# A TensorE-bound attention and MLP kernel: list-scheduled program order, DMA transposes from the seventh head pair on, exp bias as an immediate

## The chip, the cores and the metric

The kernel runs on one core of a Trainium2 chip. The metric is the device time of one execution in microseconds. A profile's span (first to last instruction) is about 2 us shorter than the time that goes with it. Engines: PE is TensorE (matmul), PEld its weight loads, DVE is VectorE, ACT is ScalarE, POOL is GpSimd, SP is SyncE, which issues DMAs here.

## The reference

Block-sparse attention over 4 batches, 8 heads, 768 tokens and head size 64 is followed by a residual token-and-channel MLP.

```python
scores = scale * q @ k.T                      # per batch and head
scores = where(mask, scores, -1e9)            # 32x32 blocks: band, edges, 3 sampled
attn = softmax(scores); x = attn @ v          # heads side by side: (4, 768, 512)
a1 = alpha1 * x + beta1
u = x + lam * (w_tok @ a1)                    # token mix, 768 x 768
a2 = alpha2 * u + beta2
out = u + lam * (relu(a2 @ w_ch1) @ w_ch2)    # channel MLP, 512 -> 2048 -> 512
```

## The kernel before

Work goes by pairs of heads, 16 in all, four to a batch. The scores of a pair are made in nine units of 1024 columns (`qk`), each goes through one exp on ScalarE (`eT`), and a second set of matmuls (`pv`) multiplies with v. The mask is added by 24 extra contraction rows of the operands: `kx` carries a block indicator, `qx` the bias of that block. After a pair come normalization, the token mix (`tok`), and a transposed copy `uT` of the result. Once a batch has all four pairs, its channel MLP runs in groups `ch1` (into `hts`, by relu) and `ch2` (into the output). All matmuls of MLP and token mix are fillers between attention units.

Both transposed operands come from TensorE, through a shared pair of PSUM buffers `mm`, and VectorE copies them out:

```python
    def prepare(b, n):                      # q and k of the next pair
        q2, k2, v2 = loaded.pop((b, n))
        ...
        for i, src in enumerate((q2, k2)):  # cast beside each other into rel
            nc.vector.tensor_copy(out=rel[:, :, :, i * D : (i + 1) * D], in_=...)
        yield
        for a in range(2):
            flat = transposes(rel, a)       # 6 matmuls against identity, into mm
            h = (2 * n + a) % NQB
            nc.vector.tensor_copy(out=qx[h][0:D, :], in_=flat[0:D, :])
            nc.vector.tensor_copy(out=kx[h][0:D, :], in_=flat[D:P, :])
            yield
```

```python
    def pair_mix(b, n):                     # cut to its end
        ...
        up = mm_tile([P, NT, P], BF)
        for t in range(NT):
            nc.tensor.transpose(up[:, t, :], ub[:, t, :], identb[:])
        nc.vector.tensor_copy(out=uTs[b][:, n, :], in_=up[:].rearrange("p o c -> p (o c)"))
```

The order is written by hand: a loop over the 144 units emits one `qk`, the `pv` of two units earlier, at most one piece of token mix, and channel groups against a credit of time. At the end `pin_order` makes the emitted order binding for every engine.

```python
    for i in range(len(units) + LAG):       # cut
        emit_qk(b, n, u)
        if u == 5: prep = prepare(*pairs[pi + 1])
        if prep is not None and u in (5, 7, 0): next(prep, None)
        ...
        if i >= NS: spent += filler(C1 if i % 2 else C2)
        ... pv of unit i - LAG ...
        spent += mix_next(i)
        if i >= NS: spent += filler(1e9)
```

The exp takes its bias from a 128x1 tile: `nc.scalar.activation(eT[:], sps[:], AF.Exp, bias=expb[:], scale=SCALE)`.

The softmax here doesn't subtract the row's maximum and nothing guards it: scores larger than these inputs give would overflow.

## Time and profile before

357.29 us is the median of three runs (352.35 to 357.5).

From the page of the kernel before: the head, some rows of the 40 slices of the span (busy tenths; PEclk is the granted TensorE clock), the chain that ended last (a name with q is a sequencer), and groups (busy us, mean ns of one, idle time before them and who ended it).

```profile
span 355.1 us, 7814 instructions
PE 333.2 (94%) x3375; PEld 220.2 (62%) x3410; DVE 210.8 (59%) x416; ACT 193.7 (55%) x213; POOL 43.4 (12%) x67
...
PE   7989998989899999999999999999999999999995
...
PEclk9999997789999999999999999999999999999999
...
PE 78%; DVE 15%; ACT 3%; issue 2%; DMA 1%; ACTq 0%; DVEq 0%
...
L299 ACT ACTIVATE eT<-sps,expb 128x1024 f16<-128x1024 f32 x144 | 157.5, 1114 | 91.4 <-PE sps L290 91.3
...
L225 PE MATMUL mm<-identb,rel 128*128 128x128 bf16 x192 | 17.3, 230 | 0.6 <-ACT hts L409 0.6
```

TensorE bounds the kernel: it is 94% busy and makes up 78% of the chain. ScalarE's exp is 1114 ns, but ScalarE waits for TensorE for 91 us, so it has room except at the start (18.5 of 20 us busy from 20 to 40 us).

Busy time of pipelined matmuls overlaps, and so says little about how much time could be won. The distance between two starts says more. The 128-column matmuls of L225 above have a mean of 230 ns each, but in the timeline such a matmul is followed after 56 ns, one of 384 after 163 ns, one of 512 after 216 ns, one of 65 after about 29 ns. I call the sum of these distances over all matmuls of the program the floor, and every start that comes later than its floor allows, an excess.

| before, us | floor | start to 50 us | 50 to 100 us | 100 to 290 us | rest | span |
|---|---|---|---|---|---|---|
| | 317.5 | 13.1 | 13.4 | 6.9 | 4.1 | 355.1 |

(Worked out from all starts in the trace; excess in each stretch; the first column of excess includes the 1.2 us before the first matmul; "rest" is nearly all the time after the last matmul. Matmuls missing from a trace, 35 here, are put back by their floor. Sums agree within 0.2 us.)

What TensorE waited for longest, in the view of waits (us in all, times, longest):

```profile
PE mm L401 <- DVE uT L383: 3.3, 6, 0.7
PE mm L382 <- DVE ub L375: 1.8, 1, 1.8
PE mm L464 <- DVE be2b L459: 1.4, 1, 1.4
```

Stretches of 20 us, in the view of windows (busy us of each engine with the number of instructions, clock, DMA share, GB/s; the share adds up packet times that can overlap, so it can exceed 1):

```profile
40.00:60.00 20.00, 18.14 (x292) 14.39 (x290) 17.23 (x39) 16.73 (x16) 8.57 (x12) 0.93 1.26 203
60.00:80.00 20.00, 17.39 (x218) 14.34 (x217) 12.93 (x26) 9.36 (x9) 2.14 (x3) 0.73 0.41 61
120.00:140.00 20.00, 19.54 (x205) 13.04 (x207) 12.87 (x26) 12.55 (x14) 2.14 (x3) 1.00 0.26 44
```

From 60 to 80 us the mean clock is 0.73. The clock record has half clock (starts of 128 columns are then 107 ns apart instead of 56) for 10.2 us from 57.2 us and for 3.4 us from 74.3 us. The two single waits above (1.4 us at 54.7 us, 1.8 us at 71.8 us) stand just before these stretches. From 100 us on there is a regular loss, 6.9 us in all. Its largest part are the six waits for uT in the list: `ch1` is queued in TensorE's order behind a q/k transpose, and waits for an `mm` buffer that the copy of uT has not yet freed (0.9 us of excess at 144, 184, 225 and 265 us).

### The profile page before, as it was taken

How to read it: one execution, taken by the hardware profiler on the slowest of the kernel's cores; microseconds unless marked ns; L12 is line 12 of the kernel's file. 1: busy time of each engine (PE TensorE's matmuls, PEld its weight loads, DVE VectorE, ACT ScalarE, POOL GpSimd, SP SyncE). 2: the span in 40 equal slices, each digit the busy share in tenths (PEclk: the TensorE clock that was granted, in tenths of full speed). 3: DMA queues.
4: the chain of work that ended last, by engine and by line, in shares of the span. 5: the costliest groups of instructions: out<-in, count | busy, mean ns of one | idle time of the engine just before them, and what ended most of it. 6: DMA issues, size and time to landing. Idle time of an engine off the chain costs nothing.

```text
span 355.1 us, 7814 instructions
## 1 busy us (share of the span) xinstructions
PE 333.2 (94%) x3375; PEld 220.2 (62%) x3410; DVE 210.8 (59%) x416; ACT 193.7 (55%) x213; POOL 43.4 (12%) x67
## 2 busy tenths in 40 slices
PE   7989998989899999999999999999999999999995
PEld 3578776765575666566666667566666656555542
DVE  3399996576785665665674755665674655242321
ACT  3898996545756656556556646566656630212110
POOL 4666334010010101002010000000000000000000
PEclk9999997789999999999999999999999999999999
DMA  5999999503132240603242000000000000001012
GB/s 132 203 220 224 207 207 201 86 3 45 22 41 30 49 78 2 99 30 50 50 54 44 31 32 0 31 31 0 31 32 0 31 31 30 31 30 61 30 40 79
DMA packets 20518, 23.34 MB, mean 66 GB/s; under 512 B 1756, under 2 KB 16260, under 8 KB 20484
## 3 DMA queue, kind: packets, MB, share of 16 engines
q0 software_dynamic: 15984, 15.47, 27.4%
q1 hardware_dynamic: 4284, 7.14, 5.6%
q8 instruction: 26, 0.43, 0.5%
q10 hardware_dynamic: 216, 0.24, 0.2%
q14 instruction: 8, 0.07, 0.1%
HBM read 30.86 MB, written 6.29 MB: 105 GB/s over the span
## 4 chain that ended last, share of the span: by engine, by line
PE 78%; DVE 15%; ACT 3%; issue 2%; DMA 1%; ACTq 0%; DVEq 0%
PE cp L433 20%; PE mm L401 19%; PE sps L290 14%; PE mm L363 8%; PE ops L311 7%; PE sps L401 3%; PE ops L433 3%; PE mm L225 2%; DVE x_sb L328 2%; ACT eT L299 2%; DVE a1p L350 2%; DVE a1p L353 1%; DVE kx L266 1%; DVE ub L375 1%; DVE x_sb L374 1%
## 5 line engine op out<-in xcount | busy, mean ns | idle before, releaser
L299 ACT ACTIVATE eT<-sps,expb 128x1024 f16<-128x1024 f32 x144 | 157.5, 1114 | 91.4 <-PE sps L290 91.3
L290 PE MATMUL sps<-qx,kx 88*128 88x512 bf16 (+1 forms) x384 | 91.0, 341 | 1.7 <-DVE kx L266 0.9
L401 PE MATMUL mm<-uT,w1b 128*128 128x384 bf16 x436 | 87.6, 325 | 4.7 <-DVE uT L383 3.3
L433 PE MATMUL cp<-w2b,hts 128*128 128x512 bf16 x303 | 78.6, 379 | 2.5 <-DVE ot L442 0.8
L401 PEld LDWEIGHTS <-w1b 128*128 128x128 bf16 x512 | 48.2, 97 | 38.9 <-issue 4.8
L311 PEld LDWEIGHTS <-eT 128*128 128x128 f16 x1152 | 56.0, 100 | 24.5 <-DVE x_sb L328 1.9
L409 ACT ACTIVATE hts<-mm,b1t 128x384 bf16<-128x384 f32 x64 | 37.0, 578 | 50.7 <-PE mm L401 50.0
L433 PEld LDWEIGHTS <-hts 128*128 128x128 bf16 x384 | 36.2, 97 | 34.2 <-issue 1.0
L311 PE MATMUL ops<-vext,eT 128*128 128x65 f16 x1008 | 53.8, 197 | 0.9 <-DVE x_sb L328 0.8
L290 PEld LDWEIGHTS <-kx 88*128 88x128 bf16 x384 | 32.4, 101 | 15.5 <-issue 2.7
L363 PE MATMUL mm<-a1p,wtokT 128*128 128x128 bf16 x576 | 41.2, 225 | 0.8 <-ACT hts L409 0.8
L363 PEld LDWEIGHTS <-wtokT 128*128 128x128 bf16 x576 | 34.8, 101 | 1.4 <-issue 0.9
L413 DVE TENSOR_SCALAR hts<-mm,b1t 128x384 bf16<-128x384 f32 x45 | 27.7, 616 | 9.1 <-PE mm L401 8.5
L374 DVE TENSOR_TENSOR x_sb<-x_sb,mm 128x384 f32<-128x384 f32 (+1 forms) x35 | 18.1, 518 | 24.3 <-PE mm L363 24.0
L265 DVE COPY qx<-mm 64x768 bf16<-64x768 bf16 x30 | 16.4, 547 | 26.2 <-PE mm L225 26.1
L442 DVE TENSOR_TENSOR ot<-x_sb,cp 128x512 f32<-128x512 f32 x21 | 14.4, 685 | 18.6 <-PE cp L433 18.6
L413 DVE TENSOR_SCALAR hts<-sps,b1t 128x384 bf16<-128x384 f32 x19 | 11.7, 617 | 20.2 <-PE sps L401 20.2
L171 POOL DMA_DIRECT2D q<-in_q_dram x15 | 10.7, 712 | 90.5 <-DVE rel L257 83.5
L325 DVE RECIPROCAL rcp<-ops 128x6 f32<-128x6 f32 x28 | 5.4, 193 | 23.2 <-PE ops L311 23.2
L375 DVE TENSOR_TENSOR ub<-x_sb,a_bc 128x384 bf16<-128x384 f32 (+1 forms) x35 | 18.3, 524 | 1.2
L225 PEld LDWEIGHTS <-rel 128*128 128x128 bf16 x192 | 14.4, 103 | 6.4 <-issue 2.9
L225 PE MATMUL mm<-identb,rel 128*128 128x128 bf16 x192 | 17.3, 230 | 0.6 <-ACT hts L409 0.6
(64 smaller groups left out, 210.4 us busy)
## 6 DMA issues: line engine op xcount, KB each, us to landing
out_dram<-ot SPq DMA_DIRECT2D x24, 256.0 KB, 2.0
v<-in_v_dram POOLq DMA_DIRECT2D x16, 192.0 KB, 5.2
q<-in_q_dram POOLq DMA_DIRECT2D x15, 192.0 KB, 6.0
k<-in_k_dram POOLq DMA_DIRECT2D x15, 192.0 KB, 6.2
w1b<-in_moe_w_ch_dram POOLq DMA_DIRECT2D x4, 512.0 KB, 10.4
w2b<-in_moe_w_ch_dram POOLq DMA_DIRECT2D x4, 512.0 KB, 15.6
wtk<-in_moe_w_tok_dram POOLq DMA_DIRECT2D x3, 384.0 KB, 8.0
a_bc<-in_moe_alpha_dram POOLq DMA_DIRECT2D x2, 256.0 KB, 8.8
```

What stands on the lines that cost most here:

```text
L225: nc.tensor.transpose(tps[:, o, :], rel[:, a, o, :], identb[:])
L265: nc.vector.tensor_copy(out=qx[h][0:D, :], in_=flat[0:D, :])
L290: nc.tensor.matmul(sps[:, f - u * UN : f - u * UN + w], kx[h][0:KC, ts(jt, P)], qx[h][0:KC, c : c + w], start=True, stop=True,)
L299: nc.scalar.activation(eT[:], sps[:], AF.Exp, bias=expb[:], scale=SCALE)
L311: nc.tensor.matmul(ops[(b, n, a)][:, t * VW : t * VW + D + 1], eTs[(b, n, u)][:, ts(c, P)], vx[:, a, jt, 0 : D + 1], start=(r == 0), stop= ...
L363: nc.tensor.matmul(tp[:, j, :], wtokT[:, s, ts(m * g + j, P)], a1p[:, s, :], start=(s == 0), stop=(s == NT - 1),)
L374: nc.vector.tensor_tensor(out=sl, in0=sl, in1=tp[:], op=ALU.add)
L375: nc.vector.tensor_tensor(out=ub[:, gs, :], in0=sl, in1=bc(a2_bc, m), op=ALU.mult)
L401: nc.tensor.matmul(hp[:, 0:HS], w1b[:, dk, ts(f, P)], uTs[b][:, dk, ts(hf, HS)], start=(dk == 0), stop=(dk == 3),)
L409: nc.scalar.activation(hts[k][:, f, :], hp[:, 0:HS], AF.Relu, bias=b1t[:, f : f + 1], scale=1.0)
L413: nc.vector.tensor_scalar(out=hts[k][:, f, :], in0=hp[:, 0:HS], scalar1=b1t[:, f : f + 1], scalar2=0.0, op0=ALU.add, op1=ALU.max,)
L433: nc.tensor.matmul(cps[k][:], hts[k][:, nk, ts(m, P)], w2b[:, nk, :], start=(nk == 0), stop=(nk == 15),)
```

## The change

It takes transposes off TensorE from the seventh pair on, and replaces the hand-written order by one that a small simulation of the engines chooses when the program is built: jobs with durations, dependencies, priorities and buffer counts, each engine always taking the best job that is ready. The relu, which went to ScalarE and VectorE in turn, now goes to the one that the simulation finds free. The exp bias becomes an immediate, and the warm-up gets 3 + 2 more matmuls.

```diff
-LAG = 2
+NPE = 6
+LEAD = 12
...
-    keep_warm(7, 512)
+    keep_warm(10, 512)
...
-    keep_warm(5, P)
+    keep_warm(7, P)
...
-        nc.scalar.activation(eT[:], sps[:], AF.Exp, bias=expb[:], scale=SCALE)
+        nc.scalar.activation(eT[:], tl.pop(("sps", p, u))[:], AF.Exp, bias=EXPB, scale=SCALE)
...
+    qs = [pp.tile([P, 2, NT, P], BF, name=f"qs{i}", tag=f"qs{i}") for i in range(2)]
+    ks = [pp.tile([P, 2, NT, P], BF, name=f"ks{i}", tag=f"ks{i}") for i in range(2)]
...
+        else:                               # pairs NPE and later
+            cq = cast_job(p, 0, "q2", ring_of(p, 0), (3, p, 0), ("ring",), ring_jobs)
+            ck = cast_job(p, 1, "k2", ring_of(p, 1), (3, p, 1), (), [cq])
...
+                def xt(p=p, a=a, h=h):
+                    for src, dst in ((qs, qx), (ks, kx)):
+                        nc.sync.dma_start_transpose(
+                            dst[h % NQB][:].rearrange("p (o c) -> p o c", o=NT),
+                            src[p % 2][:, a, :, :].rearrange("p o c -> p (o c)"))
...
+        if b == 0:                          # uT by TensorE, as before
...
+        else:
+            def uxt(p=p, n=n, ut_tile=ut_tile):
+                nc.sync.dma_start_transpose(ut_tile()[:, n, :]..., tl["ub", p][:]...)
...
-    for i in range(len(units) + LAG):       # and all of the hand-written order
+    while left:                             # list scheduling: (gated, priority) among ready jobs
+        for e in ("PE", "ACT", "DVE", "LD", "XP", "ST"):
+            ...
+            free_at[e] = t + j.dur
```

`qs` and `ks` are two staging buffers for a pair each ("the ring"): VectorE casts into them and DMA transposes read them. They also hold the mask rows, so a transpose delivers a whole `qx` or `kx`. In the changed kernel 52 DMA transposes of 192 KB go through SyncE's queue, 40 for q and k and 12 for uT.

## The prediction

> **What bounds the kernel now.** TensorE: the page has it 94% busy over 355.1 us, and the chain of waits is 78% TensorE, 15% VectorE, 3% ScalarE. Busy time overlaps, so I use distances between starts in the timeline: 56 ns for a 128-column matmul, 163 ns for 384, 216 ns for 512, about 29 ns for 65. Over all 3410 matmuls in program order that is an issue floor of 317 us. The other 38 us, each start against its floor: 13 us before 50 us (first transfers, and the half clock that the clock record holds until 16.3 us); 14 us from 50 to 100 us; 6 to 8 us of stalls from 100 to 290 us (some 1 us per head pair); almost none in the channel-only end; 4 us after the last matmul. At 50 to 100 us the clock record drops to half for 10.2 us from 57.2 and 3.4 us from 74.3, beside TensorE waits of 1.4 us (for be2b) and 1.8 us (for ub): the clock costs about 7 us.
>
> **What the change removes.** 120 q/k transposes (192 to 72) and 72 uT transposes (96 to 24): 192 x 56 ns = 10.8 us of TensorE, all critical. Added: 5 warm-up matmuls and a mask product. New floor 308 us: -10 us, nearly certain. VectorE loses 40 qx/kx copies (547 ns) and 12 uT copies (555 ns), 28.5 of 211 us; it is 96% busy from 20 to 40 us, but those copies stay (pairs 1 to 5 keep TensorE), so this helps only latency later.
>
> The exp bias as an immediate: [...] The trace has 1114 ns with the pointer[...]. Only the first 36 units feel it (ScalarE 92% busy at 20 to 40 us)[...].
>
> **What it moves.** The list-scheduled order should take most per-pair stalls (no buffer held across transpose and copy) and bring the first ch1 matmul from 78.8 us to about 65. If TensorE stays dense at 50 to 80 us the half clock does not return. I credit 7 us at 50 to 100 us, 3 us in steady state, 2 us at the start.
>
> **What it adds.** 52 DMA transposes of 192 KB on SyncE's queue, about five per 20 us pair, in order with the stores. DMA engines are about a quarter busy after 80 us; four head buffers give about a pair (20 us) of slack, so 3 to 5 us of landing time is hidden. The trace before shows no DMA transpose: this is the least known part. Above 4 us each in series the queue would become the bound.
>
> **Sum.** 355 - 10 - 7 - 3 - 2 = 333 us of span; timed runs lie 2 us above the profile: **335 us**, range **325 to 346**. Faster by over 2%: 0.91; within 2%: 0.06; slower by over 2%: 0.03.
>
> **What would show it.** Right: transposes 72 + 24 + 36, [...]no half clock after the ramp, TensorE waits for DMA-written qx/kx/uT under 3 us in total, landing of a transpose under 5 us. Wrong: TensorE waiting on those each pair; a transpose on SyncE behind a store or a buffer, holding up uT; half-clock stretches at 50 to 80 us.
>
> **What would make it wrong.** Slow or serialized DMA transposes; a fixed order that mis-times VectorE, so that TensorE stalls behind one late copy; the clock dropping in some runs and not others (before's own runs spread over 5 us), which alone moves the result by 5 us.

What makes up the 2 us at the start is not broken down. That the clock costs about 7 us is an estimate, half of the 13.6 us that the clock record of before has at half clock from 57.2 and 74.3 us. The 3 to 5 us of landing time had no trace behind them; the medians measured in the changed kernel are 2.6 us (kx), 2.7 us (uT) and 5.1 us (qx).

## The result, and the profile after

336.44 us (333.47 to 338.76, four runs, one of them slow; the three fast ones have a median of 335.49) against 354.98 us of before in the same rounds. The ratio is 0.9462 with a 95% interval of 0.9366 to 0.9558. A ratio is the mean time of one kernel's fast runs over that of the other's of the same rounds, so it is not quite the ratio of the medians. A later control of six runs gave 336.76 us and 0.9443.

The same parts of the page of the changed kernel:

```profile
span 331.7 us, 7564 instructions
PE 316.0 (95%) x3229; PEld 204.6 (62%) x3229; DVE 172.7 (52%) x352; ACT 190.4 (57%) x230; POOL 45.4 (14%) x71
...
PE   7798999896999999999999999999999999999995
...
PEclk9999999999799999999999999999999999999999
...
PE 83%; DVE 4%; ACT 4%; DMA 3%; issue 2%; SPq 1%; POOL 1%; ACTq 0%; DVEq 0%
...
L596 ACT ACTIVATE eT<-sps 128x1024 f16<-128x1024 f32 x144 | 144.5, 1024 | 69.2 <-PE sps L583 67.8
```

The transposes that are left on TensorE, in the view of groups, and the DMA transposes in the list of DMA issues (count, us to landing):

```profile
L209 PE MATMUL mm<-identb,rel 128*128 128x128 bf16 x72 | 6.0, 219 | 1.9 <-DVE rel L467 1.9
L735 PE MATMUL mm<-identb,ub 128*128 128x128 bf16 x24 | 2.0, 219 | 0.0
```

```profile
qx<-qs SPq DMA_TRANSPOSE x20, 5.1
kx<-ks SPq DMA_TRANSPOSE x20, 2.6
...
uT<-ub SPq DMA_TRANSPOSE x12, 2.7
```

q/k transposes on TensorE fell from 192 to 72. VectorE's share of the chain falls from 15% to 4%. The windows (the last row is the stretch shown of before):

```profile
60.00:80.00 20.00, 18.45 (x230) 13.06 (x227) 15.91 (x34) 13.45 (x17) 6.45 (x9) 1.00 1.38 166
80.00:100.00 20.00, 16.70 (x159) 10.91 (x160) 12.33 (x24) 8.83 (x11) 3.57 (x5) 0.91 0.83 128
120.00:140.00 20.00, 20.00 (x213) 13.08 (x212) 9.71 (x20) 11.87 (x15) 2.15 (x3) 1.00 0.56 93
```

From 100 us on TensorE is busy without a gap. The weak stretch has moved from 60 to 80 us to 80 to 100 us. Its cause heads the waits:

```profile
PE cp L816 <- DVE hts L788: 3.5, 1, 3.5
PE mm L209 <- DVE rel L467: 1.9, 1, 1.9
PE sps L583 <- DVE kx L519: 1.4, 2, 1.2
PE mm L773 <- DVE uT L738: 1.3, 1, 1.3
```

| us | floor | start to 50 | 50 to 100 | 100 to 290 | rest | span |
|---|---|---|---|---|---|---|
| before | 317.5 | 13.1 | 13.4 | 6.9 | 4.1 | 355.1 |
| changed | 307.6 | 11.5 | 7.3 | 0.5 | 4.6 | 331.7 |

So of 23 us between the two profiles, 10 are floor, 6 are in the stretch of 50 to 100 us, 6 are stalls of the steady state and 2 are from the start.

The single wait of 3.5 us deserves a look, as it is new. VectorE just before it (timeline: start, duration, what):

```profile
73.91 3.09 DVE L425 TENSOR_TENSOR w2b<-w2b,lam_bcb 128x1024 bf16<-128x1024 bf16 x5
82.35 0.36 DVE L467 COPY qs<-q 128x768 bf16<-128x768 bf16 x1 [5.35 <-issue]
82.63 0.61 DVE L788 TENSOR_SCALAR hts<-mm,b1t 128x384 bf16<-128x384 f32 x1
```

VectorE stood still for 5.35 us in front of a cast into the ring, and the relu that TensorE needed was queued behind this cast. The label "issue" only says that the view names no engine: the trace's semaphore events show that this cast waited for a DMA semaphore, that of the transpose issued at 72.55 us, and was released at 82.27 us. That transpose thus took 9.7 us to land. It was not the only one: by the same events the seven transposes issued from 65.7 to 79.0 us took 4.8 to 10.5 us. SyncE's queue at that time:

```profile
71.26 1.24 SPq L539 DMA_TRANSPOSE kx<-ks  x1
72.55 3.36 SPq L539 DMA_TRANSPOSE qx<-qs  x1
75.96 2.96 SPq L539 DMA_TRANSPOSE kx<-ks  x1
78.96 2.70 SPq L747 DMA_TRANSPOSE uT<-ub  x1
81.70 1.29 SPq L539 DMA_TRANSPOSE qx<-qs  x1
```

Most transposes of the whole run keep the queue busy for 1.2 to 1.3 us; these three take 2.7 to 3.4 us. Half clock follows for 3.4 us from 83.2 us.

### The profile page after: what moved, and what is told of

Read it like the earlier page. It is cut to its first block, busy times and chain, and to the rows that moved or that the text cites. A ratio compares the mean times of both kernels' runs of the same rounds, so it can differ in the third digit from the quotient of the medians.

```text
span 331.7 us, 7564 instructions
## 1 busy us (share of the span) xinstructions
PE 316.0 (95%) x3229; PEld 204.6 (62%) x3229; DVE 172.7 (52%) x352; ACT 190.4 (57%) x230; POOL 45.4 (14%) x71
## 4 chain that ended last, share of the span: by engine, by line
PE 83%; DVE 4%; ACT 4%; DMA 3%; issue 2%; SPq 1%; POOL 1%; ACTq 0%; DVEq 0%
PE mm L773 22%; PE cp L816 21%; PE sps L583 15%; PE mm L698 9%; PE ops L621 8%; PE ops L816 4%; ACT eT L596 4%; DMA wtk<-in_moe_w_tok_dram 2%; PE sps L773 1%; SPq L539 1%; DMA tab<-tab_c 1%; DVE w2b L425 1%; DVE kx L519 1%; PE cp L621 1%; PE mm L209 1%
## 5 line engine op out<-in xcount | busy, mean ns | idle before, releaser
L596 ACT ACTIVATE eT<-sps 128x1024 f16<-128x1024 f32 x144 | 144.5, 1024 | 69.2 <-PE sps L583 67.8
L773 PE MATMUL mm<-uT,w1b 128*128 128x384 bf16 x488 | 96.9, 327 | 1.3 <-DVE uT L738 1.3
L784 ACT ACTIVATE hts<-mm,b1t 128x384 bf16<-128x384 f32 x75 | 43.5, 580 | 58.0 <-PE mm L773 56.8
L833 DVE TENSOR_TENSOR ot<-x_sb,cp 128x512 f32<-128x512 f32 x20 | 13.7, 686 | 38.1 <-PE cp L816 37.9
L708 DVE TENSOR_TENSOR x_sb<-x_sb,mm 128x384 f32<-128x384 f32 x32 | 17.7, 552 | 19.9 <-PE mm L698 18.9
L276 POOL DMA_DIRECT2D v<-in_v_dram x16 | 11.6, 727 | 49.0 <-DVE vext L564 44.6
L714 DVE TENSOR_TENSOR ub<-x_sb,a_bc 128x384 bf16<-128x384 f32 x32 | 17.7, 555 | 0.8
L816 PE MATMUL ops<-w2b,hts 128*128 128x512 bf16 x64 | 16.4, 379 | 0.0
L648 DVE TENSOR_TENSOR x_sb<-ops,rcp 128x384 f32<-128x384 f32 x28 | 15.6, 557 | 1.0
L678 DVE TENSOR_TENSOR a1p<-x_sb,a_bc 128x768 bf16<-128x768 f32 (+1 forms) x20 | 15.9, 793 | 0.3
L686 DVE TENSOR_TENSOR a1p<-a1p,b_bc 128x768 bf16<-128x768 bf16 (+1 forms) x20 | 15.8, 790 | 0.2
## 6 DMA issues: line engine op xcount, KB each, us to landing
w2b<-in_moe_w_ch_dram POOLq DMA_DIRECT2D x4, 512.0 KB, 15.2
a_bc<-in_moe_alpha_dram POOLq DMA_DIRECT2D x2, 256.0 KB, 10.1
```

The source lines that it names most:

```text
L596: nc.scalar.activation(eT[:], tl.pop(("sps", p, u))[:], AF.Exp, bias=EXPB, scale=SCALE)
L678: nc.vector.tensor_tensor(out=tl["a1p", p][:, :, lo : lo + w], in0=x_sb[:, s0 : s0 + NT, c : c + w], in1=bc(a1_bc, NT, c, w), op=ALU.mult,)
L686: nc.vector.tensor_tensor(out=t, in0=t, in1=bc(b1_bc, NT, c, w), op=ALU.add)
L708: nc.vector.tensor_tensor(out=sl, in0=sl, in1=tl.pop(("tp", p, g))[:], op=ALU.add)
L714: nc.vector.tensor_tensor(out=tl["ub", p][:, 3 * g : 3 * g + 3, :], in0=sl, in1=bc(a2_bc, 3, 2 * n * D, P), op=ALU.mult,)
L773: nc.tensor.matmul(hp[:, 0:HS], w1b[:, dk, ts(f, P)], uTs[b][:, dk, ts(hf, HS)], start=(dk == 0), stop=(dk == 3),)
```

## The experiments

Medians are quoted with the median of before in the same rounds, since chips and rounds differ by some 4 us.

The table has all profiled runs in the form used above; the arguments below point to it.

| us | floor | start to 50 | 50 to 100 | 100 to 290 | rest | span |
|---|---|---|---|---|---|---|
| e1: new order, TensorE transposes | 318.2 | 13.9 | 2.9 | 0.4 | 4.3 | 339.8 |
| e6: old order, DMA transposes (faulty) | 306.3 | 12.8 | 8.7 | 4.9 | 4.4 | 337.2 |
| e6b: the same, mended | 306.7 | 13.0 | 10.1 | 4.9 | 4.4 | 339.0 |
| e4: before, immediate | 317.5 | 13.1 | 10.7 | 6.6 | 4.1 | 352.1 |
| e5: before, long warm-up (a slow run) | 318.2 | 15.2 | 13.7 | 6.9 | 4.1 | 358.2 |
| e2: changed, pointer bias | 307.6 | 12.5 | 8.7 | 1.2 | 4.6 | 334.6 |
| e3: changed, short warm-up | 307.1 | 14.4 | 4.5 | 1.1 | 4.6 | 331.7 |
| g1: changed, loads held back | 307.4 | 14.2 | 2.3 | 0.5 | 4.6 | 328.9 |
| g2: changed, three staging buffers | 307.6 | 14.5 | 11.7 | 0.6 | 4.6 | 339.0 |
| c1: changed again | 307.4 | 15.1 | 5.4 | 0.6 | 4.6 | 333.0 |
| g4: three buffers and held back | 307.4 | 14.6 | 2.2 | 0.5 | 4.6 | 329.4 |
| g5: held back, one pair earlier | 306.8 | 13.7 | 5.0 | 0.5 | 4.3 | 330.3 |

### e1: the new order with all transposes on TensorE

```diff
-NPE = 6
+NPE = 16
...
-        if b == 0:
+        if True:
```

> The changed kernel, but every transpose back on TensorE (the order is listed anew by the same engine model). Theory (the removed matmuls are worth their issue time, and the order is worth the rest): 192 x 56 ns = 10.8 us more TensorE floor, so about 346 us, still 8 to 10 us under before; the chain stays dense after 100 us (stalls under 1 us). Rival (the DMA transposes also took the stalls, because their copies and mm buffers were what TensorE waited for): 350 us or more, with about 1 us of stalls per pair as before. A third possibility: the 3.5 us stall at 79 us and the half clock behind it come from the DMA transposes themselves; then this kernel has neither and lands near 342 us.

341.49 us against 354.85 us, ratio 0.9635 (0.957 to 0.970). The profile has all 192 matmuls back (3421, floor 318.2 us) and the steady state is as dense as with DMA transposes: 0.4 us of excess from 100 to 290 us. So the per-pair stalls do not need DMA transposes to go; the order alone removes them. The third possibility came true: the stall at 80 us is absent (2.9 us of excess from 50 to 100 us instead of 7.3), no half clock appears after 17.4 us, and the time is near its 342 us. The order (with the immediate and the longer warm-up, which this kernel keeps) is worth 13 us here, and DMA transposes in this order only about 6 (the two ratios, of different rounds, differ by 1.7%), not much over half of the 10.6 us of floor that they remove.

### e6: the old order with DMA transposes

```diff
+        if pi >= NPE:
+            for src, st_ in ((q2, qs), (k2, ks)):
+                nc.vector.tensor_copy(out=st_[pi % 2][:, :, :, 0:D], in_=...)
+            yield
+            for a in range(2):
+                h = (2 * n + a) % NQB
+                for st_, dst in ((qs, qx), (ks, kx)):
+                    nc.sync.dma_start_transpose(dst[h][:]..., st_[pi % 2][:, a, :, :]...)
+                yield
+            return
...
+        if b > 0:
+            nc.sync.dma_start_transpose(uTs[b][:, n, :]..., ub[:]...)
+            yield 0, 3
+            return
...
-            if prep is not None and u in (5, 7, 0):
+            if prep is not None and u in ((1, 2, 3) if dma else (5, 7, 0)):
```

> The kernel before with its hand-written order, pointer bias and warm-up, but with DMA transposes from the seventh pair on (prepared four units earlier, so that they can land) and for uT of the last three batches. Theory: 10 us of TensorE floor go and the per-pair stalls behind qx/kx/uT copies go too (5 us), while the start and the half clock at 57 us stay: 338 to 343 us. Rival (the hand order cannot place the late landings): uT waits of 2 to 4 us per pair appear and the gain is under 6 us, 348 us or more.

337.75 us against 354.85 us, ratio 0.9505 (0.9415 to 0.9595). A count of its matmuls showed a fault: 66 q/k transposes instead of 72. With the last line of the edit, the step at u = 0 fell out where the old way hands over to the new, so the second head of the sixth pair kept an older head's q and k. The scores are so small that the result still passed. The mended kernel, e6b, keeps that step:

```diff
-            if prep is not None and u in ((1, 2, 3) if dma else (5, 7, 0)):
+            if prep is not None and u in ((0, 1, 2, 3) if dma else (5, 7, 0)):
```

> The hand order with DMA transposes once more, mended: in the first version the second head of the sixth pair was never transposed (66 instead of 72 q/k transposes in its program; the output passed the comparison all the same, since the scores are small). The six matmuls and two copies that were missing are worth about 0.5 us on TensorE. Theory (the missing work was small): 336 to 341 us, ratio 0.945 to 0.96. Rival (the gap flattered it): over 343 us.

340.6 us (336.7 to 341.23, six runs) against 354.42 us, ratio 0.96 (0.9537 to 0.9663). That is within the range of both theories. The rival of e6 falls: the hand order placed the late landings without a wait for uT. The waits of e6b:

```profile
PE cp L466 <- DVE ot L475: 2.1, 3, 0.8
PE mm L497 <- DVE be2b L492: 1.4, 1, 1.4
```

The wait for uT that headed the list of before is gone; other small ones stay (4.9 us of excess from 100 to 290 us instead of 6.9, so 2 us went and not the 5 that I expected), and so do the wait for be2b at 54 us and the half clock after it, 13.7 us from 56.6 us.

Together e1 and e6b make a table of two by two, with the ratio to before in their own rounds:

| ratio to before (median us) | TensorE transposes | DMA transposes |
|---|---|---|
| hand order | 1 | 0.960 (340.6) |
| list-scheduled order | 0.9635 (341.49) | 0.9462 (336.44) |

The lower row also has the immediate and the longer warm-up. e4 and e5 below find no gain from either in the hand order, but e2 leaves some us of the immediate open in the listed order; what is called the order here includes that. The order alone is then worth 3.7%, DMA transposes alone 4.0%, and both together 5.4% (5.6% in the control) instead of 7.7%. About 2% is missing, 7 to 8 us. Two candidates: stalls that either change removes can be won only once, and the new stall at 80 us exists only where both are present. The experiments g1 and g4 below size the second.

### e4 and e5: the immediate and the longer warm-up in the kernel before

```diff
-        nc.scalar.activation(eT[:], sps[:], AF.Exp, bias=expb[:], scale=SCALE)
+        nc.scalar.activation(eT[:], sps[:], AF.Exp, bias=EXPB, scale=SCALE)
```

> The kernel before with the exp bias as an immediate, nothing else. Theory: exp falls from 1114 to about 1024 ns, ScalarE is not on the chain after 60 us, so the time falls by 0 to 2 us (36 units x 90 ns = 3.2 us at most, hidden partly behind VectorE). Rival (ScalarE sets the pace of batch 0): 3 us or more.

```diff
-    keep_warm(7, 512)
+    keep_warm(10, 512)
...
-    keep_warm(5, P)
+    keep_warm(7, P)
```

> The kernel before with the longer warm-up alone (10 and 7 matmuls). Theory (the warm-up brings the full clock at about 5 us instead of 16 us): the clock record starts at full by 6 us, TensorE's excess over its floor before 20 us falls by about 3 us, and the time by 1 to 3 us (part is hidden because ScalarE and transfers bound the start). Rival: the moment of the full clock is luck of the run; no difference beyond the spread.

The immediate: 354.45 against 354.85 us, ratio 0.9992 (0.9908 to 1.0077). Exp fell from 1114 to 1023 ns, and nothing came of it. The warm-up: 356.75 us, ratio 1.0035 (0.9935 to 1.0135). It did bring the full clock at 6.1 us instead of 16.3 us. But in the profiled run VectorE's copy of wtokT then held TensorE for 2.6 us at 22.3 us, half clock came for 6.8 us from 26.6 us, and the gain was gone. That profiled run is of state slow, so only the time, from fast runs, carries the verdict: no gain.

### e2 and e3: the same two, taken out of the changed kernel

The edits are those of e4 and e5 in reverse.

> The changed kernel with the exp bias through the pointer again; instruction order unchanged. Theory: exp back at about 1114 ns; only the first 36 units are near ScalarE's pace, so 0 to 3 us slower, 336 to 339 us; TensorE waits for exp before 50 us grow (they are about 1 us in all in the changed kernel). Rival (new order keeps TensorE so dense that ScalarE latency never shows): no difference beyond 1 us.

> The changed kernel with the old warm-up (7 and 5 matmuls). In the kernel before the longer warm-up alone gave nothing (356.8 against 354.9 us): full clock at 6 us instead of 16, but a half-clock window later at 27 us. Theory (warm-up only trades where the cold microseconds fall, since the start waits for transfers and ScalarE): within 2 us of 336 us. Rival (in the new order the early full clock is worth its 2.7 us of excess before 20 us): 339 us or more.

With the pointer: 338.98 us against 352.5 us, ratio 0.9602 (0.9547 to 0.9658), so perhaps 2 to 5 us slower than the changed kernel, whose ratio is 0.9462 in other rounds. Exp is 1117 ns again. The result is not clean: the stall at 80 us happened to be 4.7 us long in the profiled run. The excess from 20 to 50 us alone, where ScalarE is near the pace, was 5.3 us against 3.9 to 4.3 us in all profiled runs of the new order with the immediate. About 1 us is therefore what I put down to the immediate, and the rest stays open.

With the short warm-up: 335.7 us, ratio 0.9511 (0.9461 to 0.956): no different from the changed kernel. Its clock was at half until 16.9 us, against 4.7 us in the first profile of the changed kernel, and both profiles have the same span of 331.7 us. In the control c1, with the long warm-up, full clock came at 6.2 us, and half clock returned for 6.8 us from 13.1 us. The warm-up moved the cold time in these runs; a gain from it is not seen.

### g1: the loads held back

Theory A: the transposes near 75 us were slow because q, k and v loads were in flight beside them. Between 65.9 and 71.5 us the POOL queue had started six loads of 192 KB, for pairs 10 and 11, as soon as buffers came free; the first scores of pair 10 come at 159 us. Then the queue waited 10.7 us for the stalled cast:

```profile
65.87 0.71 POOL L276 DMA_DIRECT2D q<-in_q_dram  x1 [2.95 <-DVE qs L467]
...
71.54 0.75 POOL L276 DMA_DIRECT2D v<-in_v_dram  x1
83.01 0.72 POOL L276 DMA_DIRECT2D q<-in_q_dram  x1 [10.72 <-DVE qs L467]
```

By their semaphores these six loads landed between 72.1 and 81.5 us. Rival B: several queued transposes are slow by themselves. Dependencies in the build-time model only fix the order in a queue and do not delay a load, so the experiment adds a real one: a token that VectorE writes after normalizing pair p, and that POOL must read before it starts the loads of pair p + 3.

```diff
+                if a == 1 and p >= 6:
+                    nc.vector.memset(tokt[:, p : p + 1], 1.0)
+                    nc.gpsimd.tensor_copy(out=hold2[:, p : p + 1], in_=tokt[:, p : p + 1])
...
+    for p in range(9, len(pairs)):
+        for nm in ("q2", "k2", "v2"):
+            ld[p, nm].deps.append(norm[p - 3, 1])
+            ld[p, nm].lat = 5000.0
```

> The changed kernel, with the q, k and v loads of pairs 9 to 15 really held back on the POOL queue, each until the pair three before it is normalized (a tiny token copy). Theory A (the transposes between 72 and 82 us took 2.7 to 3.4 us each to issue and about 10 us to land because bulk loads were in flight beside them; VectorE's copy into the transpose ring waited for one of them, 5.3 us, and TensorE 3.5 us behind a relu queued after it): their issue falls to the usual 1.2 us, landings to under 6 us, the 3.5 us TensorE stall at 79 us and the half clock behind it go, and the time falls by 4 to 5 us, to about 331 to 333 us. Rival B (several transposes queued at once are slow by themselves): issues stay at 3 us, the stall and 336 us stay.

330.03 us against 352.5 us, ratio 0.9358 (0.9327 to 0.939). SyncE's queue in g1, in the same stretch:

```profile
73.88 1.22 SPq L541 DMA_TRANSPOSE kx<-ks  x1
75.15 1.28 SPq L541 DMA_TRANSPOSE qx<-qs  x1
76.48 1.29 SPq L541 DMA_TRANSPOSE kx<-ks  x1
77.81 1.29 SPq L752 DMA_TRANSPOSE uT<-ub  x1
```

The same three transposes, just as tightly queued, now take 1.3 us each, which refutes B as the cause of this stall. All nine transposes issued from 68.3 to 82.1 us landed after 2.5 to 3.9 us. VectorE's cast no longer waits:

```profile
79.52 0.35 DVE L469 COPY qs<-q 128x768 bf16<-128x768 bf16 x1
80.45 0.62 DVE L793 TENSOR_SCALAR hts<-mm,b1t 128x384 bf16<-128x384 f32 x1 [0.58 <-PE mm L778]
```

The windows of g1:

```profile
60.00:80.00 20.00, 18.60 (x249) 14.15 (x249) 18.46 (x41) 13.73 (x17) 0.00 (x0) 1.00 0.58 97
80.00:100.00 20.00, 19.90 (x205) 13.14 (x206) 11.43 (x21) 11.61 (x15) 0.00 (x0) 1.00 0.28 67
```

The DMA share from 60 to 80 us is 0.58 instead of 1.38, TensorE is busy for 19.9 of 20 us from 80 us on instead of 16.7, and the clock stays full. The list of waits no longer has the wait for `hts`. The excess from 50 to 100 us is 2.3 us, 5.0 less than in the changed kernel. One side effect: the casts of pair 9 and later move back a little in VectorE's order, because the model now knows of the later loads. At the stall itself VectorE's order is the same in both traces (five w2b, cast, relu, cast), so this is not what removed it.

### g2: a third staging buffer

```diff
-    slots = dict(..., ring=2, ...)
+    slots = dict(..., ring=3, ...)      # and qs, ks of three tiles; eqt shares a1_bc's space
```

> The changed kernel with three instead of two staging buffers between the cast and the DMA transpose (a scratch tile shares space to make room). Under A and B alike the copy into the ring for the third DMA pair no longer waits for the first pair's transposes, so the 3.5 us TensorE stall at 79 us should go: 331 to 334 us. If the stall only moves to the next pair's copies or to qx/kx themselves arriving late, 335 us or more.

340.44 us against 352.5 us, ratio 0.9651 (0.9615 to 0.9687): slower than the changed kernel, by 4 us by the medians or 1.9% by the ratios (other rounds), not faster. I had expected any version without the wait on the first pair's transposes to win. Its waits and SyncE's queue:

```profile
PE cp L816 <- DVE hts L788: 7.1, 1, 7.1
```

```profile
76.45 4.53 SPq L539 DMA_TRANSPOSE qx<-qs  x1
81.02 3.60 SPq L539 DMA_TRANSPOSE kx<-ks  x1
84.66 3.70 SPq L747 DMA_TRANSPOSE uT<-ub  x1
```

The third buffer lets a third pair be cast at once, which frees load buffers earlier, and the POOL queue starts eight loads from 69 to 77.3 us instead of six. The transposes get slower still (issue up to 4.5 us, landing up to 12.5 us), and the wait moves one pair on and doubles. It is the same mechanism with a larger dose.

### c1, g4 and g5: a control, both together, and one pair earlier

> The changed kernel once more, as a control beside the versions with held-back loads on the same chip. Theory: about 336 us, its runs spread over 3 us or more with the clock (0.98 to 0.995), a stall of 2 to 5 us in front of the second matmul group at about 80 us in the profile. If it lands within 2 us of the version with held-back loads (330 us), the gain of that one was the chip's.

> Three staging buffers and held-back loads together. With three buffers alone the time rose to 340.4 us and the stall to 7.2 us, I think because the third buffer let more loads start at once. Theory A (load contention is the cause, not the ring): with the loads held back the transposes issue in 1.2 us again, no stall over 2 us at 80 us, 329 to 332 us. Rival (the third buffer itself, or the changed order that it gives, costs the time): 335 us or more.

> Held-back loads, and DMA transposes one pair earlier (from the sixth pair on). 12 transposes fewer on TensorE: 0.7 us of floor. Theory A says that the sixth pair's transposes, at about 60 to 66 us, run beside the loads of pairs 6 to 8 that are still in flight there, so some of them take 2 us or more to issue, and TensorE waits for qx or kx: no gain or a loss of 1 to 4 us against 330 us. If they run at 1.2 us each: 329 to 330 us.

All three in the same five rounds, with before at 356.86 us: c1 336.76 us, ratio 0.9443 (0.9372 to 0.9513); g4 331.01 us, 0.9297 (0.9238 to 0.9356); g5 331.36 us, 0.9317 (0.9257 to 0.9376).

The control repeats the changed kernel, the stall included (3.2 us at 82.8 us), though here no half clock follows it. g4 settles the third buffer: with the loads held back it costs nothing and gains nothing over g1. The load traffic was the cause, not the buffer. g4 beats both kernels in the same rounds, the changed one by 5.7 us; g1 did so against before, in other rounds.

With the loads held back, order and DMA transposes together give 6.4% (g1) and 7.0% (g4). Of the 2% that were missing from 7.7%, the new stall thus accounts for 0.9 to 1.5%. What is left, 0.6 to 1.3%, fits stalls that can be won only once, but it is no larger than the intervals, so this last part is not shown.

g5 removes 12 more matmuls from TensorE and gains nothing. Its waits show why:

```profile
PE sps L585 <- DMA kx<-ks: 2.2, 2, 2.1
```

This is the only profile in which TensorE itself waits long for a DMA-written operand. Thirteen transposes stand in a row from 61.8 to 79.8 us in SyncE's queue; TensorE waited for the last of them, which landed at 82.3 us, and half clock follows for 3.4 us from 83.0 us. Two of them took 2.2 and 2.1 us to issue although no q, k or v load had started since 57.9 us (the last of these landed at 65.2 us). So loads are not the only thing that slows a transpose, and my expectation, which named loads, is not confirmed. The cause was not varied, but the trace has a candidate: a DMA packet of 16 KB on queue q8, of kind instruction, ran for 1.5 us from 68.2 us and for 1.0 us from 78.2 us. In g5 all 16 slow transposes away from loads (issue over 1.5 us or landing over 3.4 us) overlap such an instruction packet (16 or 8 KB); of the 27 others 7 do.

### What the clock adds to the spread

The four first runs of the changed kernel, time and mean clock: 333.47 us at 0.995, 335.49 at 0.990, 337.39 at 0.985, and 338.76 at 0.983 (slow). If the lower clock is all half clock, as in the clock records, 0.995 is 3.3 us at half clock and 0.985 is 10.1 us (share below 1, times 2, times the span); the time of these two fast runs differs by 3.9 us for 6.8 us more of half clock. All of g1's four runs lie within 1.2 us, at 0.990 to 0.995. But the mean clock does not settle the time (two fast runs of c1, both at 0.990, took 334.79 and 337.43 us), and a stall does not always bring half clock: none followed the 3.2 us of c1 or the 1.9 us that e3 has at the same place, while 10.2 us of it followed a wait of 1.4 us in the kernel before. I have not varied the clock by itself, so what it costs is not shown.

## Why the prediction was right or wrong

The time, the range and the class were right: 335 us predicted, 336.44 us measured. That the sum came so close is partly luck, since two errors nearly cancel: the steady state gave 3.4 us more than its term, and a stall that the prediction did not have cost some 5 us. Taken by its terms:

- **Floor, "-10 us, nearly certain": right.** 317.5 to 307.6 us, with the predicted 72 + 24 + 36 transposes in the program.
- **"3 us in steady state": mechanism right, too small.** The excess from 100 to 290 us fell from 6.9 to 0.5 us, by 6.4 us. I credited the order with half of the stalls; it took nearly all of them, as e1 shows without any DMA transpose.
- **"7 us at 50 to 100 us": size about right (6.1 us), the reason only in part.** ch1 came forward from 78.7 to 63.9 us, as predicted (65), and the waits for be2b and ub, with the half clock after them, went. But "the half clock does not return" failed in the profiled run: it returned for 3.4 us behind a stall that the change itself made. Where the stretch stayed dense it did not come: e1 (2.9 us of excess) had no half clock after 17.4 us, g1 (2.3 us) a mean clock of 1.00 from 60 to 100 us. Without that stall this term would have been 11 us (g1 and g4).
- **"2 us at the start": right in the profiled run (1.6 us), but not a robust gain.** c1 has 15.1 us before 50 us, more than the 13.1 of before. The warm-up alone brought no gain that the runs show, in either kernel.
- **The exp: 1024 ns measured.** With the bias as an immediate an exp took 91 ns less in the kernel before (1114 to 1023, e4) and 93 less in the changed one (1117 to 1024, e2). In time that gave nothing in the kernel before, and about 1 us that I put down to it in the new order.
- **DMA transposes, "3 to 5 us of landing time is hidden", "landing under 5 us": wrong in one stretch.** uT landed in 2.7 us, kx in 2.6 and qx in 5.1 us in the median, of those landings that the trace could tie to their issue. But that leaves out most of the slow ones: beside the bulk loads the seven issued from 65.7 to 79.0 us took 4.8 to 10.5 us. I had read off that the DMA engines are a quarter busy after 80 us, in the profile of *before*. The first transposes run at 65 to 80 us, and the new order also started loads in a burst there: the DMA share from 60 to 80 us rose from 0.41 to 1.38 (0.58 with these loads held back).
- **"TensorE waits for DMA-written qx/kx/uT under 3 us": true to the letter, and it missed the path.** TensorE never waited for them directly in the changed kernel. VectorE did, for a staging buffer that a transpose had not yet read, and VectorE's fixed order passed 5.35 us of that on to TensorE as 3.5 us.
- **What the prediction did not say** is that order and DMA transposes overlap. It counted them as separate terms. By themselves they are worth 3.7% and 4.0%, together 5.4%.

No run here failed the comparison, but e6 shows that the comparison can miss a wrong q or k, so it does not prove every transposed operand right.

## What to carry to other kernels

When two changes each free the same bottleneck, test them two by two: here either alone gave about 4%, and both together only 5.4%. When a fixed order has one engine feed both a DMA and the bottleneck engine, ask for each of its instructions what it can be held up by: a staging copy that waited 5.35 us for a DMA to read its buffer held up the relu queued behind it, and TensorE for 3.5 us. Loads that started as soon as a buffer was free came in a burst here, six between 65.9 and 71.5 us; tie loads to real progress of the computation when latency-critical DMAs run beside them, for this was worth another 5.7 us here (g4 against c1).

## What the runs measured of the hardware

- An SBUF-to-SBUF DMA transpose of 128x768 in two bytes kept SyncE's queue for 1.21 us (uT) to 1.28 us (kx) and landed after 2.7 and 2.6 us, all medians of the changed kernel.
- With six loads of 192 KB in flight, seven transposes took 4.8 to 10.5 us to land and three of them 2.7 to 3.4 us to issue; with eight loads issue rose to 4.5 us (g2); with the loads held back, the same three took 1.3 us each (g1). The six loads themselves took 5.8 to 10.0 us to land.
- In g5 all 16 slow transposes away from loads overlap a DMA packet of kind instruction (told above; a coincidence in time, not an experiment).
- In streams of weight load and matmul pairs, TensorE's starts were 56 ns apart for 128 columns and 216 ns for 512, in both traces.
- Ten warm-up matmuls instead of seven brought full clock at 4.7 us (changed), 6.1 us (e5) and 6.2 us (c1) instead of 16.3 us (before) and 16.9 us (e3), but in e5 and c1 half clock came back for 6.8 us, from 26.6 and 13.1 us, and neither kernel became faster (ratio 1.0035 in e5, 335.7 us without it in e3).
